# A fixed instruction list is replaced by another: merged exponentials, work moved to GpSimd, another loading order

## The chip, the cores and the metric

The kernel runs on one core of a Trainium2 chip. The metric is the device time of one execution in microseconds (us). Three runs of the kernel before took 295.99, 296.73 and 299.36 us; the median is 296.73.

## The reference

One transformer layer on 2048 tokens of width 640, bfloat16. Attention has 32 heads of width 20 and goes through four segments of 512 tokens. Each segment combines ordinary causal softmax attention inside the segment with a read from a memory matrix that earlier segments have filled; then comes an MLP with hidden width 1728.

```
x -> layernorm -> q, k, v = x@wq, x@wk, x@wv          (32 heads of 20)
phi(t) = t + 1 if t > 0 else exp(t);  g = sigmoid(beta)
for each segment s of 512 tokens:
    a_dot = softmax(q k^T * 20**-0.5 + causal mask) v
    a_mem = (phi(q) M) / (phi(q) z + 1e-6)
    o[s]  = g * a_mem + (1 - g) * a_dot
    M += phi(k)^T v ;  z += sum(phi(k))
h   = x + o @ wo
out = h + silu(layernorm(h) @ w1) @ w2
```

## The kernel before

All work is cut into named tasks. Each task is a few instructions on one engine. The order of the tasks is not computed in the kernel: it stands in a long text, `ORDER`, which names one task after another. `Graph.schedule` walks through it. An entry reads `name/engine:slots`. The engine letter is A (ScalarE, ACT), D (VectorE, DVE), G (GpSimd, POOL) or S (SP, which issues the DMAs); without a letter the first engine that the task allows is taken. The letter C on a TensorE task means the same matmuls cut into four column tiles of 32 (line 549) instead of the whole array (line 548). The numbers are buffer slots; for the pool `ps` they are PSUM banks, of which there are eight. Every engine carries out its own tasks in the order of the list. A tracker puts a semaphore wait wherever a task reads or overwrites what another engine made. So a task that waits holds up everything behind it on its engine, and the list is the whole plan.

The tasks by name, with s the segment, c one of five blocks of packed heads, b one of 16 blocks of 128 tokens, k = 8s + g the group of four heads:

- `x0` to `x12`, `w_...`: loads of tokens and weights; `re_...` rearranges query and key weights into the packed form; `fillN` is N small matmuls on zeros.
- `n1_stb`, `n1_rsb`, `n1_apb`: layer-norm statistics (line 753; on ACT lines 744 to 748), reciprocal root on GpSimd (763, 765) and application (781). For the first segment the result is transposed by TensorE (`n1_tp`, 791) and copied (`n1_te`, 800), later by a transposing DMA (`n1_tr`). `n2_...` is the same before the MLP.
- `prscw` (548, 549) projects queries (w = 0) or keys (w = 1), `qescw` evicts (876, 877). `ex` (883), `pa` (the clamp max(t, 0) + 1, line 890) and `pb` (896) make phi. `vt` are DMAs that bring the heads of groups 5 to 7, split over the blocks, together (the virtual heads).
- `v`, `ve`: value projection and its eviction (842, 843).
- `qk{k}a`, `qk{k}b`, `qk{k}e`: a score visit, eight or four matmuls in four row tiles (946) into four banks, two pairs. `e{k}a0` and `e{k}a2` are the exponentials of the two pairs (959). `mk` sets the upper triangle of the diagonal blocks to zero on GpSimd (971).
- `av` multiplies by the values (994, "PV product" below), `oe` evicts with the gate (1008 on ACT, 1010 on DVE), `tm` and `td` bring memory and local result to token order, `nm` normalizes (1058 to 1064), `ad` adds the two (1072, GpSimd).
- `kt`, `mz`, `ma`, `mb`: the memory update.
- `ot`, `wo`, `rs`: output projection and residual; `h1` and `th` (1211), `s` (1217): first MLP product and SiLU through tanh; `h2`, `o` (1254), `out`: second product, last addition, store.

In the list the MLP of segment s runs between the score visits of segment s + 1 and s + 2, so that TensorE has matmuls to do while ACT works through the exponentials. The last segment's MLP stands alone at the end.

The exponential of a pair is one instruction over two banks:

```
def e_ex(eng, q0=q0, scp=scp):
    b0 = scp.slot
    T.add(AC, lambda e: e.activation(out=pt[:, pta.slot, q0:q0 + 2, 0:width],
                                     in_=sc3[:, b0:b0 + 2, 0:width], func=ACT.Exp, scale=SCALE), ...)
```

Of the kernel before, what the change touches and what calls it, by code (L numbers as in the profile page):

```python
# [6 lines left out]
ALU = mybir.AluOpType  # L7
# [220 lines left out]
class Task:  # L228
    __slots__ = ("name", "engs", "emit", "reads", "writes", "prio", "mode", "allocs", "preds", "npred",
                 "succ", "ready", "lat", "start", "end", "eng", "idx", "bw", "cols", "alt")  # L230
# [4 lines left out]
class Graph:  # L235
# [15 lines left out]
    def task(self, name, engs, emit, reads=(), writes=(), prio=0.0, mode=None, reserve=(), lat=None, bw=0.0, alt=False):  # L251

        t = Task()
        t.cols, t.alt = False, alt
# [33 lines left out]
    def schedule(self):  # L288
# [3 lines left out]
        for row in ORDER:  # L292
# [18 lines left out]
            for a in t.allocs:  # L311
# [7 lines left out]
            for a in t.allocs:  # L319
                a.users -= 1  # L320
# [54 lines left out]
pr030.1/C qe040/D pa031:0 av0:3 pb021 mk1a qe030/D mm1 n1_tr7 vt05 oe0/D:0 qk2e0:6,4 vt010 mk1b av1:2 e2b2 epsg1 mk2b
pb041 mk2a td0/C:3 e2e2:5 e2e0 oe1/D:1 qk3a0:4,0 nm0:3,0 vt07 e3a2:6 v10.0:2 td1:6 nm1:2 vt011 e3a0 v10.1 ve10/D:1
qk3b0:0,6 e3b2:4 e3b0 mm7 n1_st9:2 mk2e av2:3 mk3a oe2/D:1 qk4a0:6,4 e4a2:3 v11.0/C:2 e4a0 v11.1/C qk4b0:0,4 td2/C:6
epsg0 ve11/D pb031 mk3b nm2:2 mtb3 av3:7 e4b0:1 vt01 e4b2 vt02 n1_rs9 oe3/D:0 mzc1 n1_st10:7 vt08 n1_st8:1 vt04
qk4e0:2,0 mk4a pr100.0/C:4 e4e2:4 pr100.1/C qe100/D:0 pa100:0 qk5a0:0,6 pr110.0/C:5 pr110.1/C e4e0 qe110/D:0 e5a0:5
w_wo/S:0 qk5b0:2,0 pr120.0/C:4 pr120.1/C qe120/D:0 mk4b e5a2 mk4e av4:5 oe4/D:1 mk5a kt02:0 pa120:0 e5b2:2 qk6a0:0,6  # L380
n1_rs8 td3/C:4 n1_ap8:0 nm3:0 e5b0 mk5b v12.0:2 v12.1 kt04:4 ve12/D e6a0:1 ex120:0 e6a2 w_w2_3/S td4:1 ex100:1 mz01:0
mz00 mm8 mz04 mz02 kt03:1 n1_rs10 n1_ap10:3 mz03 ma0/D:0 qk6b0:4,2 e6b2:0 e6b0 mk6b nm4:3 pr101.0:7 pr101.1 qk6e0:0,2
e6e2:6 qe101/D av5:6 pr111.0/C:7 pr111.1/C e6e0 qk7a0:4,2 mk6e w_w2_0/S mk6a e7a0:4 e7a2 n1_tr8:1 mk7a oe5/D:0 qe111/D
td5:6 pr130.0/C:0 pr130.1/C nm5:1 n1_tr10 qk7b0:6,4 e7b2:5 e7b0 mk7b n1_ap9:0 qe130/D:0 n1_st11:7 v13.0:1 mm3 v13.1/C
ve13/D ex101:2 n1_rs11 av6:0 qk8a0:3,6 e8a0:3 pa101:0 e8a2 pr140.0:5 pr140.1/C av7:4 oe6/D:1 mzc3 qk8b0:0,2 w_w1_4/S
td6/C:6 e8b0:2 w_w1_3/S n1_tr9 mzc5 pb101 kt10:1 qe140/D:0 oe7/D:0 mk8a nm6:2 pr131.0/C:7 td7/C:4 nm7:1 mzc7 mzc4
ot0:0 qk8e0:5,0 pr131.1/C ot1 n1_ap11:1 mm0 qe131/D pr121.0:4 pr121.1 pa130:0 pa110:0 ot2 qe121/D vt19:0 pa131:1 mzc0
e8b2 mk8b e8e0:5 w_w2_4/S mzc2 qk9a0:5,2 pb100 e8e2 mk8e pr141.0:7 pr141.1 qe141/D pa121:0 e9a2:4 qk9b0:0,2 e9a0 pb120
pa111:2 wo0.0/C:4 wo0.1/C rs0 e9b0:6 av8:7 e9b2 vt12 mk9b ot3 ex110:0 wo1.0/C:0 qk10a0:3,5 oe8/D:0 n1_tr11 vt16
n2_st0:1 vt10 e10a0:3 wo1.1 rs1 n2_st1:6 mb00:0 mm11 vt13 e10a2 wo2.0:2 wo2.1 rs2 ex111:2 pb111 n2_st2:0 mk10a  # L390
qk10b0:6,0 e10b2:0 vt11 wo3.0/C:4 wo3.1/C qk10e0:2,0 rs3 vt15 n2_rs1 e10b0 vt14 v21.0:6 e10e2:2 vt18 n2_ap1:0 n2_st3:6
e10e0 v21.1 ve21/D:0 mm9 qk11a0:4,0 e11a0:1 mm6 n2_tr1:0 v20.0/C:2 v20.1/C n2_rs0 v22.0/C:4 n2_rs2 tm8/C:6 td8/C
ex131:2 ex130:1 n2_ap2:3 ve20/A n2_tr2 v22.1/C e11a2 mk10b pb110 pr201.0/C:2 n2_rs3 n2_ap3:1 n2_tr3 nm8:0,1 n2_ap0:2
n2_tr0 ex121:0 mk9a pb130 av9:3 ve22/A qk11b0:6,0 e11b0:5 pr201.1 qe201/D:0 oe9/D:1 v23.0:4 v23.1 mk10e mb02:0 av10:2
e11b2 mb01:0 ve23/A qk12a0:0,6 mzc8 td9:4 pb121 ex141:0 tm9 pa140:0 vt110 e12a2:4 pr211.0:3 pr211.1 oe10/D:0 td10:6
e12a0 tm10 h1_0_0_0.0:2 qe211/A:0 mk11a pb131 h1_0_0_0.1 th0_0_0:0 ad8:0 nm9:0,1 mk11b mzc6 qk12b0:3,0 mb03:0 e12b2:0
nm10:1,0 av11:5 s0_0_0:0 h1_0_1_0.0/C:6 e12b0 h1_0_1_0.1/C kt11:4 pa141:2 pr221.0/C:7 vt111 vt17 qk12e0:2,0 w_w2_1/S
th0_1_0:0 pr221.1 oe11/D:1 tm11:4 td11 s0_1_0 ex140:1 e12e0:2 h1_0_2_0.0:6 h1_0_2_0.1 pb141 kt14:0 qe221/D:0 e12e2
# [924 lines left out]
```

## Time and profile before

| | |
|---|---|
| runs | 295.99, 296.73, 299.36 us |
| span of the profiled execution, first to last instruction | 293.9 us (the median of the runs is 2.8 above it; no separate time is listed for the profiled execution) |
| PE busy | 282.0 us (96%), 4365 matmuls |
| weight loads (PEld) | 159.8 us (54%) |
| DVE busy | 218.6 us (74%), 456 instructions |
| ACT busy | 216.5 us (74%), 281 |
| POOL busy | 148.1 us (50%), 294 |
| chain that ended last | PE 83%, DVE 7%, ACT 6%, DMA 1%, issue 1% |
| granted TensorE clock | full |

The page gives busy time by engine, then the span in 40 slices, the DMA queues, the chain of work that ended last, and groups of instructions with their mean duration and what ended the idle time before them. Matmuls are pipelined, and a matmul's recorded length covers its way through the array, so PE counts as busy over short waits. A wait is put down to the engine that released it last; "issue" means that the trace shows nothing that was waited for.

### The profile page before, as it was taken

To read this page: it belongs to the slowest core of one execution; us is meant where nothing else is said; L and a number is where in the kernel's file an instruction comes from. 1 tells how busy PE (TensorE), PEld (TensorE's weight loads), DVE (VectorE), ACT (ScalarE), POOL (GpSimd) and SP (SyncE) were. 2 spreads that over 40 slices of the span, in tenths; PEclk is the share of its full clock that TensorE was granted. 3 is DMA by queue.
4 is the path that set the end of the run, shared out by engine and by line. 5 is a ranking of instruction groups with operands and counts; after the bars stand their busy time and mean duration, and the time that the engine had idled before them with its cause. 6 is when DMAs were issued, how large, how long until landed. Compare 5 with 4: busy or idle time off the path is not lost.

```text
span 293.9 us, 10138 instructions
## 1 busy us (share of the span) xinstructions
PE 282.0 (96%) x4365; PEld 159.8 (54%) x4365; DVE 218.6 (74%) x456; ACT 216.5 (74%) x281; POOL 148.1 (50%) x294
## 2 busy tenths in 40 slices
PE   6899889999999999999999899999999999999996
PEld 5454435445644445566654554656664657754574
DVE  3999888899997678798899835877746776635613
ACT  7699999999999899977789857979979640005400
POOL 6759675686947545746748432348638321300000
PEclk9999999999999999999999999999999999999999
DMA  7947869635464200453543402403320031450003
GB/s 212 342 120 186 113 176 186 167 69 108 87 80 113 73 2 3 53 99 70 91 122 92 93 2 21 81 2 57 73 25 2 2 70 22 91 156 0 3 0 112
DMA packets 48604, 24.83 MB, mean 84 GB/s; under 512 B 38896, under 2 KB 47472, under 8 KB 48560
## 3 DMA queue, kind: packets, MB, share of 16 engines
q1 hardware_dynamic: 48560, 24.19, 38.1%
q8 instruction: 34, 0.56, 0.8%
q14 instruction: 10, 0.08, 0.1%
HBM read 10.41 MB, written 2.62 MB: 44 GB/s over the span
## 4 chain that ended last, share of the span: by engine, by line
PE 83%; DVE 7%; ACT 6%; DMA 1%; issue 1%; POOL 0%; SPq 0%; ACTq 0%; DVEq 0%
PE ps_all L548 49%; PE ps_all L549 20%; PE ps_all L946 8%; ACT PT L959 5%; PE ps_all L994 5%; DMA x_tok<-in_A_x_dram 1%; PE ps_all L1198 1%; DVE xn_rot L781 1%; DVE oTs L1010 1%; DVE phiQ L890 1%; DVE stt L753 1%; PE ps_all L1112 1%; DVE Vx L843 1%; DVE otok L1046 1%; DVE QK L877 0%
## 5 line engine op out<-in xcount | busy, mean ns | idle before, releaser
L959 ACT ACTIVATE PT<-ps_all 128x1024 bf16<-128x1024 f32 x160 | 154.1, 1027 | 16.2 <-PE ps_all L946 15.1
L971 POOL TENSOR_SCALAR_AFFINE_SELECT PT<-PT 128x512 bf16<-128x512 bf16 x128 | 82.8, 651 | 63.9 <-ACT PT L959 60.5
L1211 ACT ACTIVATE th<-ps_all 128x512 f32<-128x512 f32 (+1 forms) x56 | 31.7, 589 | 38.1 <-PE ps_all L548 23.7
L1217 DVE SCALAR_TENSOR_TENSOR sT<-th,ps_all 128x512 bf16<-128x512 f32 (+1 forms) x56 | 36.0, 661 | 17.0 <-ACT th L1211 16.4
L548 PE MATMUL ps_all<-w_sb,sT 128*128 128x320 bf16 x324 | 46.3, 299 | 0.1
L548 PE MATMUL ps_all<-tT,w_sb 128*128 128x512 bf16 x178 | 41.4, 380 | 0.0
L548 PEld LDWEIGHTS ps_all<-w_sb,sT 128*128 128x128 bf16 x324 | 31.0, 98 | 13.2 <-issue 0.6
L753 DVE BATCH_NORM_STATS2 stt<-x_tok 128x6 f32<-128x320 bf16 x62 | 27.1, 478 | 3.8 <-DMA x_tok<-in_A_x_dram 3.6
L1072 POOL TENSOR_TENSOR otok<-on 128x320 bf16<-128x320 bf16 x24 | 19.7, 824 | 17.5 <-DVE on L1064 17.5
L1254 DVE SCALAR_TENSOR_TENSOR x_tok<-ps_all,x_tok 128x640 bf16<-128x640 f32 (+1 forms) x17 | 13.3, 784 | 17.9 <-PE ps_all L548 13.1
L548 PEld LDWEIGHTS ps_all<-tT,w_sb 128*128 128x128 bf16 x178 | 16.5, 98 | 18.7 <-issue 0.6
L877 DVE CAST QK<-ps_all 128x512 bf16<-128x512 f32 x25 | 17.1, 685 | 8.6 <-PE ps_all L548 4.7
L1010 DVE TENSOR_SCALAR oTs<-ps_all,lsc 128x512 bf16<-128x512 f32 x26 | 19.3, 741 | 2.6 <-PE ps_all L994 2.2
L549 PE MATMUL ps_all<-tT,w_sb 128*32 128x512 bf16 x328 | 20.5, 380 | 0.0
L1064 DVE TENSOR_TENSOR on<-ps_all,rd 128x640 bf16<-128x640 f32 x24 | 19.8, 824 | 0.8
L765 POOL TENSOR_TENSOR rst<-rst,eps_c 128x1 f32<-128x1 f32 x32 | 18.3, 573 | 2.5
L549 PE MATMUL ps_all<-w_sb,sT 128*32 128x320 bf16 x496 | 18.8, 300 | 0.0
L781 DVE TENSOR_SCALAR xn_rot<-x_tok,mvt,rst 128x640 bf16<-128x640 bf16 x31 | 16.1, 534 | 3.3 <-POOL rst L765 2.8
L548 PE MATMUL ps_all<-tT,wkr 128*128 128x512 bf16 (+1 forms) x77 | 18.4, 367 | 0.0
L548 PE MATMUL ps_all<-wv_sb,tT 128*128 128x320 bf16 x115 | 18.0, 300 | 0.5 <-ACT PT L959 0.3
L763 POOL TENSOR_TENSOR rst<-mvt,eps_c 128x1 f32<-128x1 f32 x32 | 6.7, 209 | 22.5 <-DVE mvt L756 21.8
L994 PE MATMUL ps_all<-PT,Vx 128*32 128x512 bf16 (+3 forms) x384 | 17.4, 301 | 0.0
(111 smaller groups left out, 403.1 us busy)
## 6 DMA issues: line engine op xcount, KB each, us to landing
out_dram<-x_tok SPq DMA_DIRECT2D x15, 160.0 KB, 1.9
w_sb<-in_B_w_dram SPq DMA_DIRECT2D x5, 432.0 KB, 4.1
x_tok<-in_A_x_dram SPq DMA_DIRECT2D x3, 640.0 KB, 4.4
w_sb<-in_B_w_dram SPq DMA_DIRECT2D x3, 480.0 KB, 4.0
QKV<-QK SPq DMA_DIRECT2D x12, 72.0 KB
wv_sb<-in_A_wv_dram SPq DMA_DIRECT2D x1, 800.0 KB, 8.2
wo_sb<-in_A_wo_dram SPq DMA_DIRECT2D x1, 800.0 KB, 5.3
w_sb<-in_B_w_dram SPq DMA_DIRECT2D x1, 640.0 KB, 6.0
```

What stands on the lines that cost most here:

```text
L548: return [lambda e: e.matmul(out, lhsT=lhsT, rhs=rhs, start=start, stop=stop)]
L549: return [lambda e, p=p: e.matmul(out[p:p + 32, :], lhsT=lhsT[:, p:p + 32], rhs=rhs, start=start, stop=stop, tile_position=(0, p)) for p i ...
L753: T.add(DV, lambda e, hh=hh: e.bn_stats(out=stt[:, s, 6 * hh:6 * hh + 6], in_=xb[:, 320 * hh:320 * hh + 320]), reads=R((xa, xsub)), writes ...
L946: fns.append(lambda e, j=j, o=o, r=r, q0=q0, q1=q1, qa=qa, ka=ka: e.matmul(ps_all[:, o:o + q1 - q0], lhsT=ka[32 * r:32 * r + DH, 128 * j:1 ...
L959: T.add(AC, lambda e: e.activation(out=pt[:, pta.slot, q0:q0 + 2, 0:width], in_=sc3[:, b0:b0 + 2, 0:width], func=ACT.Exp, scale=SCALE), re ...
L971: fns.append(lambda e, v=v: e.affine_select(out=v, in_=v, pattern=[[0, 4], [1, 128]], compare_op=ALU.is_ge, fill=0.0, base=0, channel_mult ...
L994: fns.append(lambda e, j=j, r=r, h=h, pa=pa, pt=pt, co=co, q0=q0, ji=ji: e.matmul(bank(po)[32 * r:32 * r + 32, q0:hi], lhsT=vtile(vx)[:, j ...
L1010: f = lambda e: e.tensor_scalar(out=o, in0=i_, scalar1=lsc[:, g:g + 1], scalar2=None, op0=ALU.mult)
L1064: T.add(DV, lambda e: e.tensor_tensor(out=on[:, ona.slot, :, :].rearrange("p b (x e) -> p b x e", e=DH), in0=v[:, :, :, 0:DH], in1=r2.unsq ...
L1072: T.add(PO, lambda e: e.tensor_tensor(out=o_dst, in0=on[:, ona.slot, 0, :].rearrange("p (i x) -> p i x", i=4), in1=on[:, ona.slot, 1, :].r ...
L1211: T.add(AC, lambda e: e.activation(out=th[:, tha.slot, lo:hi], in_=bank(ps)[:, lo:hi], func=ACT.Tanh, scale=0.5), reads=R((ps, [0])), writ ...
L1217: T.add(DV, lambda e: e.scalar_tensor_tensor(out=sT[:, f, lo:hi], in0=th[:, tha.slot, lo:hi], scalar=1.0, in1=bank(ps)[:, lo:hi], op0=ALU. ...
```

## The change

The list is another one from the first entry to the last. What it uses and the code now offers:

- 19 score visits have one exponential over all four banks instead of two over a pair each. The letter W on one of the two tasks takes the other in; the pairs are then sorted by bank, and one access pattern with the distance between them reads both.
- Clamps `pa` and applications `n1_ap`, `n2_ap` may run on GpSimd. In the list 16 of 30 clamps and 15 of 32 applications do. The ACT form of the very first application, with its extra GpSimd instruction for the bias, is gone.
- The leading fillers are 20 and 5 instead of 25 and 5.
- Entries with C for TensorE are 283 instead of 116.
- The loads at the start come in another order: x block 0, blocks 2 and 3, block 1, key weights, query weights, beta, value weights; before: blocks 0, 1, 2 and 3, query weights, key weights, value weights, beta.

The same matrix products are computed. The core of the diff, with the two lists cut to their first lines:

```diff
@@ schedule
-            t.cols = eng == "C"
-            t.eng = {"A": AC, "D": DV, "G": PO, "S": SP, "C": PE}[eng] if eng else list(t.engs)[0]
+            t.cols, t.whole = eng == "C", eng == "W"
+            t.eng = {"A": AC, "D": DV, "G": PO, "S": SP, "C": PE, "W": AC}[eng] if eng else list(t.engs)[0]
+            both = [t]
+            if t.whole:
+                m = todo.pop(name[:-1] + ("2" if name[-1] == "0" else "0"))
+                both.append(m)
...
@@ ORDER
-epsc:0 iota halfc zpad warm:0 x0:0 mt2 n1_st0:4 mt3 mt0 mt1 mta1 mtb1 vpad1 x1:1 n1_st1/A:1,2 x2:2,3 w_q0:0 w_q1 w_k0
-vpad0 fill25:0 n1_rs0 n1_ap0/A:1 sel n1_tp0:2 fill5:7 n1_te0/A:1 n1_st2/D:5,3 mta0 n1_rs1 n1_st3:0 n1_rs2 w_k1 w_wv:0
...
+zpad:0 x0:1 vpad1 warm:0 mt1 mta1 iota n1_st0:1 sel x2:7,0 n1_st2:7,0 fill20:7 mt2 epsc mta2 mtb2 mt3 mta3 mm10 halfc
+n1_rs0 mt0 n1_ap0/G:1 fill5:6 n1_st3:0 x1:2 n1_st1/A:2,2 n1_rs1 n1_tp0:3 n1_te0:2 n1_ap1 n1_tp1:0 n1_te1 n1_rs2 n1_ap2
+n1_tp2:4 n1_te2 n1_rs3 n1_ap3:2 n1_tp3:6 n1_te3 w_k1:0 w_k0 re_wk3/G:0 re_wk1/G mtb3 mm11 re_wk0 pr001x.0/C:2 w_q1
...
@@ layer_norm
-            if eng == AC:
-                T.add(AC, lambda e: e.activation(out=xn_rot[:, xn.slot, :], in_=x_tok[:, b % 12, :], func=ACT.Identity,
-                                                 scale=rst[:, s, :], bias=nmr[:, s, :]),
...
-        G.task(f"{tag}ap{b}", {DV: 0.46, AC: 0.70} if first else {DV: 0.46}, e_apply,
+        G.task(f"{tag}ap{b}", {DV: 0.46, PO: 0.88}, e_apply, [(xa, xsub), (st, ["mv", "r"])], [(xn, [0])], prio)
...
@@ declare_front
-                    G.task(f"pa{s}{c}{w}", {DV: 0.37}, e_pa, [(qk[c], wall)], [(pa, ["a"])], prp)
+                    G.task(f"pa{s}{c}{w}", {DV: 0.37, PO: 0.7}, e_pa, [(qk[c], wall)], [(pa, ["a"])], prp)
...
@@ scores
+                        if any(t.whole for t in ets):
+                            a, b = rank()
+                            src = bass.AP(tensor=ps_all, offset=512 * a.slot,
+                                          ap=[[4096, 128], [512 * (b.slot - a.slot), 2], [512, 2], [1, width]])
+                            o = pt[:, pta.slot, 0:4, 0:width].rearrange("p (a b) x -> p a b x", a=2)
+                            T.add(AC, lambda e: e.activation(out=o, in_=src, func=ACT.Exp, scale=SCALE), ...)
+                            return
```

(The numbers in braces in the code are the planner's costs; the fixed list does not read them.)

More of the change, by code (lines that the diff above doesn't have):

```diff
@@ L229 @@
     __slots__ = ("name", "engs", "emit", "reads", "writes", "prio", "mode", "allocs", "preds", "npred",
-                 "succ", "ready", "lat", "start", "end", "eng", "idx", "bw", "cols", "alt")
+                 "succ", "ready", "lat", "start", "end", "eng", "idx", "bw", "cols", "alt", "whole")
 class Graph:
@@ L253, in task @@
         t = Task()
-        t.cols, t.alt = False, alt
+        t.cols, t.alt, t.whole = False, alt, False
         t.name, t.emit, t.mode, t.lat, t.bw = name, emit, mode, lat, bw
@@ L318, in schedule @@
             assert not slots, name
-            for a in t.allocs:
-                a.users -= 1
+            for q in both:
+                for a in q.allocs:
+                    a.users -= 1
             order.append(t)
@@ L733, in layer_norm @@
         xn = G.alloc("xn")
-        first = tag == "n1_" and b < 1
         if tag == "n1_":
@@ L766, in e_rstd @@
                   reads=R((st, ["r"]), (C, ["half"])), writes=R((st, ["r"])))
-            if first:
-                T.add(PO, lambda e: e.tensor_scalar(out=nmr[:, s, :], in0=mvt[:, s, 0:1], scalar1=rst[:, s, :], scalar2=-1.0,
-                                                    op0=ALU.mult, op1=ALU.mult),
-                      reads=R((st, ["mv", "r"])), writes=R((st, ["n"])))
-        G.task(f"{tag}rs{b}", {PO: 0.83}, e_rstd, [(st, ["mv"]), (C, ["eps", "half"])],
-               [(st, ["r", "n"] if first else ["r"])], prio)
+        G.task(f"{tag}rs{b}", {PO: 0.83}, e_rstd, [(st, ["mv"]), (C, ["eps", "half"])], [(st, ["r"])], prio)
         def e_apply(eng):
             s = st.slot
-            if eng == AC:
-                T.add(AC, lambda e: e.activation(out=xn_rot[:, xn.slot, :], in_=x_tok[:, b % 12, :], func=ACT.Identity,
-                                                 scale=rst[:, s, :], bias=nmr[:, s, :]),
-                      reads=R((xa, xsub), (st, ["r", "n"])), writes=R((xn, [0])))
-                return
-            T.add(DV, lambda e: e.tensor_scalar(out=xn_rot[:, xn.slot, :], in0=x_tok[:, b % 12, :],
-                                                scalar1=mvt[:, s, 0:1], scalar2=rst[:, s, :],
-                                                op0=ALU.subtract, op1=ALU.mult),
+            T.add(eng, lambda e: e.tensor_scalar(out=xn_rot[:, xn.slot, :], in0=x_tok[:, b % 12, :],
+                                                 scalar1=mvt[:, s, 0:1], scalar2=rst[:, s, :],
+                                                 op0=ALU.subtract, op1=ALU.mult),
                   reads=R((xa, xsub), (st, ["mv", "r"])), writes=R((xn, [0])))
-        G.task(f"{tag}ap{b}", {DV: 0.46, AC: 0.70} if first else {DV: 0.46}, e_apply,
-               [(xa, xsub), (st, ["mv", "r", "n"] if first else ["mv", "r"])], [(xn, [0])], prio)
+        G.task(f"{tag}ap{b}", {DV: 0.46, PO: 0.88}, e_apply, [(xa, xsub), (st, ["mv", "r"])], [(xn, [0])], prio)
         if tag == "n1_" and b < 4:
@@ L955, in scores, with e_ex @@
                     scp = sca[(q0 - r0) // 2]
-                    def e_ex(eng, q0=q0, scp=scp):
+                    def e_ex(eng, q0=q0, scp=scp, rank=rank, ets=ets):
+                        if any(t.whole for t in ets):
+                            a, b = rank()
+                            src = bass.AP(tensor=ps_all, offset=512 * a.slot,
+                                          ap=[[4096, 128], [512 * (b.slot - a.slot), 2], [512, 2], [1, width]])
+                            o = pt[:, pta.slot, 0:4, 0:width].rearrange("p (a b) x -> p a b x", a=2)
+                            T.add(AC, lambda e: e.activation(out=o, in_=src, func=ACT.Exp, scale=SCALE),
+                                  reads=[("ps", z.slot + q) for z in (a, b) for q in range(2)], writes=R((pta, [0, 2])))
+                            return
                         b0 = scp.slot
```

215 lines of the change are left out of this document (111 added, 104 removed).

## The prediction

> **What bounds the kernel now.** I began with the page (span, engines, chain), went to the busy time by stretch, then to the chain in order of time, and last to single groups and to the first 14 us.
>
> ```profile
> span 293.9 us, 10138 instructions
> ...
> PE 282.0 (96%) x4365; PEld 159.8 (54%) x4365; DVE 218.6 (74%) x456; ACT 216.5 (74%) x281; POOL 148.1 (50%) x294
> ...
> PE 83%; DVE 7%; ACT 6%; DMA 1%; issue 1%; POOL 0%; SPq 0%; ACTq 0%; DVEq 0%
> ```
>
> TensorE is 96% busy and is 83% of the chain that ended last. The matmuls' amount does not change, so I ask where TensorE stands still. I cut the span at the first score visit (13.47), at the visits of groups 8 and 17, and behind the last group's PV product, and call the five stretches rows one to five. Columns: PE, weight loads, DVE, ACT, POOL busy; clock; DMA.
>
> ```profile
> 0.00:13.47 13.47, 9.87 (x75) 6.85 (x76) 8.25 (x33) 9.50 (x16) 9.46 (x36) 1.00 0.86 266
> 13.47:57.61 44.14, 40.78 (x713) 20.47 (x713) 39.31 (x87) 42.22 (x52) 29.95 (x65) 1.00 0.78 169
> 57.61:118.12 60.51, 59.69 (x1135) 30.57 (x1132) 52.05 (x107) 57.42 (x74) 39.02 (x74) 1.00 0.33 65
> 118.12:231.90 113.78, 112.31 (x2038) 65.07 (x2039) 85.64 (x174) 94.33 (x119) 64.37 (x109) 1.00 0.32 57
> 231.90:293.90 62.00, 59.39 (x416) 36.81 (x412) 33.35 (x60) 13.05 (x24) 5.32 (x11) 1.00 0.20 54
> ```
>
> The granted clock is full everywhere. PE idles 3.36 us in the second row, 0.82 in the third, 1.47 in the fourth; the 2.6 of the last row is the closing add and store. ACT is 96% and 95% busy in rows two and three: there PE and ACT are both at their limit, and PE's waits are ACT's length showing through. So at most 5.65 us of visible idle can go, plus waits under some 0.15 us that pipelined matmuls cover in this view, plus changes of PE's mode. Those I price from the chain (start, length):
>
> ```profile
> 37.24 3.79 ACT PT L959 x4
> ...
> 42.76 1.19 PE ps_all L549 x20
> 43.95 0.33 PE ps_all L946 x8
> ...
> 63.91 1.19 PE ps_all L548 x5
> ...
> 104.63 2.27 PE ps_all L549 x40
> ...
> 291.33 0.49 DVE x_tok L1254
> ```
>
> Five 512-column steps ahead of a visit take 1.19, ten take 2.27: five more cost 1.08, so one change of mode costs 0.11. Whole-array (L548) and four-column-tile form (L549) cost the same, 1.19 each.
>
> **The change, part by part.**
>
> *Mode changes and column tiles.* In the two written lists PE changes mode 173 times before and 165 after: 8 x 0.11 = -0.9 us (bounds -1.0, and 0 if a wait fills the place). The tail turns to column tiles almost throughout, at the same price per step. But each step is then four matmuls: 4365 become 6397.
>
> *Fillers.* 20 and 5 in place of 25 and 5; they end before the transposes need PE. 0, since the chain below waits for data.
>
> *Merged exponentials.* Prices by group (mean ns):
>
> ```profile
> L959 ACT ACTIVATE PT<-ps_all 128x1024 bf16<-128x1024 f32 x160 | 154.1, 1027 | 16.2 <-PE ps_all L946 15.1
> L971 POOL TENSOR_SCALAR_AFFINE_SELECT PT<-PT 128x512 bf16<-128x512 bf16 x128 | 82.8, 651 | 63.9 <-ACT PT L959 60.5
> ...
> L1211 ACT ACTIVATE th<-ps_all 128x512 f32<-128x512 f32 x52 | 30.3, 604 | 35.6 <-PE ps_all L548 23.7 <-DVE sT L1217 11.4 <-PE ps_all L549 0.4
> ...
> L1072 POOL TENSOR_TENSOR otok<-on 128x320 bf16<-128x320 bf16 x24 | 19.7, 824 | 17.5 <-DVE on L1064 17.5
> ...
> L781 DVE TENSOR_SCALAR xn_rot<-x_tok,mvt,rst 128x640 bf16<-128x640 bf16 x31 | 16.1, 534 | 3.3 <-POOL rst L765 2.8 <-DVE sT L1217 0.4
> L883 ACT ACTIVATE ex<-QK 128x512 bf16<-128x512 bf16 x25 | 15.5, 630 | 1.2 <-DVE phiQ L896 1.2
> ...
> L890 DVE TENSOR_SCALAR phiQ<-QK 128x512 bf16<-128x512 bf16 x15 | 7.1, 491 | 0.1
> ...
> L1008 ACT ACTIVATE oTs<-ps_all,lsc 128x512 bf16<-128x512 f32 x6 | 4.1, 690 | 0.1
> ...
> L711 POOL COPY wkr<-sT 128x400 bf16<-128x400 bf16 x2 | 1.1, 563 | 1.3 <-DMA sT<-in_A_wk_dram 1.3
> ```
>
> 512 more elements cost 1027 - 604 = 423 ns, so 1024 more cost 846 and a merged exponential 1.87. Two in a row cost 1.95: four take 3.79, hence 0.92 each and 1.03 the last. Saved: 0.08. Upper bound the whole fixed part, 1027 - 846 = 0.18; lower bound -0.1, since a merged one starts after all eight matmuls (0.33 a visit) and frees no bank at half time. I take 0.08: 19 x 0.08 = 1.5 us of ACT, two in row two, seven in row three, ten in row four.
>
> *Moves on ACT.* The list shifts three clamp exponentials (L883) out of row two, one to before it and two into row three: with the merges, row two loses 3 x 0.6 + 0.16 = 2.0, row three gains 2 x 0.6, one eviction (L1008, 0.69) and loses 0.56: +1.3. Row four gains two evictions and loses ten times 0.08, +0.6, where ACT has 19 idle: nothing. Of row two's 2.0 I count half, since DVE (39.31 of 44.14) and the masks then end last: **-1.0** (bounds -2.0, +2.0). Row three: PE has only 0.82 idle, ACT 3.1; **+0.2** (-0.8, +1.3).
>
> *Clamps and applications on GpSimd.* 16 clamps and 15 applications leave DVE: 16 x 0.49 + 14 x 0.53 = 15 us of 218.6 (the fifteenth application was on ACT). On GpSimd no such row exists. Lower bounds: the select (651 ns for 512), 0.65 and 0.81; upper: the two-input add (824 for 320), 1.32 and 1.65. Both are one-input operations like the copy (563 for 400), so I take 0.72 and 0.90: +25 us on an engine with 146 idle. That is nothing on the path where masks keep their lead over the PV products, and 2 to 4 us where they lose it (a rival). For DVE the relief counts in row four, where it frees 6 clamps and 9 applications, 7.7 of 85.64.
>
> DVE's own clamps and applications are uneven:
>
> ```profile
> L781 DVE TENSOR_SCALAR xn_rot<-x_tok,mvt,rst x31: 433/442/911, 7.9 to 257.2; 128x640 bf16<-128x640 bf16 x31
> ```
>
> Minimum 433, longest 911. The Trainium skill, "SBUF — State Buffer", section "Who interferes with whom", says that such a DVE operation and a GpSimd instruction hold a shared port pair exclusively, the loser blocking wholly. The spread agrees with it but no row names the blocker. By that rule a busier GpSimd delays what stays on DVE; by the mean row it does not. With half of the 31 stretched by 0.47 the sum would lose 7 of DVE's 15, and the rival below gains weight.
>
> *Row four.* Its idle holds one stop in the middle of a visit:
>
> ```profile
> 168.80 0.23 PE L946 MATMUL ps_all<-QKV 20*128 20x128 bf16 x3 [0.88 <-issue]
> ```
>
> Nothing in the trace released it; I read it as instructions that had not arrived. It need not fall on a dense place again: I count half, -0.45. Of the other 0.59 and the covered small waits I take -1.05, because DVE has 7.7 us more room. Row four: **-1.5** (-2.5, +1.5).
>
> *The head.* SP's loads are ordered anew: block 1 of x after blocks 2 and 3, key weights before query weights.
>
> ```profile
> 3.59 0.74 ACT L744 ACTIVATE xn_rot<-x_tok 128x640 bf16<-128x640 bf16 x1 [0.23 <-DMA x_tok<-in_A_x_dram]
> 5.61 0.92 ACT L777 ACTIVATE xn_rot<-x_tok,nmr,rst 128x640 bf16<-128x640 bf16 x1
> 5.88 0.88 DVE L753 BATCH_NORM_STATS2 stt<-x_tok 128x6 f32<-128x320 bf16 x2 [1.56 <-DMA x_tok<-in_A_x_dram]
> ...
> 8.08 0.32 POOL L763 TENSOR_TENSOR rst<-mvt,eps_c 128x1 f32<-128x1 f32 x1 [0.18 <-DVE mvt L756]
> ...
> 9.22 0.45 DVE L781 TENSOR_SCALAR xn_rot<-x_tok,mvt,rst 128x640 bf16<-128x640 bf16 x1 [0.51 <-POOL rst L765]
> 9.73 0.45 PE L791 MATMUL ps_all<-ident,xn_rot 128*128 128x128 bf16 x5 [0.51 <-DVE xn_rot L781]
> 10.08 0.71 PE L548 MATMUL ps_all<-tT,wqr 128*128 128x256 bf16 x5
> 10.45 1.06 POOL L711 COPY wkr<-sT 128x400 bf16<-128x400 bf16 x3 [1.33 <-DMA sT<-in_A_wk_dram]
> 13.47 0.39 PE L946 MATMUL ps_all<-w_sb 20*128 20x512 bf16 x4
> ```
>
> Today block 1 is there at 3.59 and its statistics on ACT end at 5.61 (2.02). Loaded third it lands when the third load does, 5.88, and ends at 7.9. On GpSimd the reciprocal roots of blocks 1, 2 and 3 stand behind it in order, 0.8 each (8.08 to 9.12 with the gap to L781): 10.3. The last application ends at 10.75 and its transposes at 11.2, where today they end at 10.18. First projection 11.1 against 10.08; the query weights, now the last of the four to land, come near 10.45 and are hidden. The same projections stand before the first visit in both lists: 14.6 against 13.47, **+1.1** (bounds +0.4 if block 1 lands with x's bytes at once, +1.8 if an early rearrangement is late too).
>
> *SP's queue otherwise.* The loads of blocks 4 to 11 come as two issues in a row right behind the attention weights, and the output weight's load now stands ahead of the copies of the virtual heads, which group 5 is the first to need. One issue more in that queue is covered by the visits of groups 0 to 4; without that cover group 5's first visit would wait as long as the issue takes. 0.
>
> **Sum:** +1.1 - 0.9 - 1.0 + 0.2 - 1.5 = -2.1. Span 293.9 - 2.1 = 291.8. The median of the runs is 296.73, 2.8 above the span, and that stays: **294.6 us**.
>
> **Rivals.**
>
> *The list closes nearly all gaps.* All 5.65 of idle but a floor of 0.5, and 0.9 of mode changes, against +1.1: -5.0, **291.8**. For it: half of DVE's relief falls where PE waits; against it: row two has every engine near its limit.
>
> *Masks come late (slower).* Place: groups 2 to 5, row two, where GpSimd does its work in order.
>
> ```profile
> 37.43 1.34 POOL L971 TENSOR_SCALAR_AFFINE_SELECT PT<-PT 128x512 bf16<-128x512 bf16 x2 [1.38 <-ACT PT L959]
> 42.92 1.34 POOL L971 TENSOR_SCALAR_AFFINE_SELECT PT<-PT 128x512 bf16<-128x512 bf16 x2 [0.50 <-ACT PT L959]
> ...
> 39.41 0.72 PE L994 MATMUL ps_all<-PT,sT 128*32 128x512 bf16 x16
> 45.30 0.72 PE L994 MATMUL ps_all<-PT,sT 128*32 128x512 bf16 x16
> ```
>
> ```profile
> 13.47:45.30 31.83, 28.85 (x433) 14.09 (x436) 28.48 (x65) 30.58 (x38) 23.04 (x52) 1.00 0.72 166
> ```
>
> Masks end at 38.77 and 44.26; the PV products that need them start at 39.41 and 45.30, a lead of 0.64 and 1.04. Up to 45.30 GpSimd idles 31.83 - 23.04 = 8.8 us, of which the two waits shown for exponentials, 1.9, stay: 6.9 of room. The new list puts three clamps and three applications more there: 3 x 0.72 + 3 x 0.90 = 4.9 us at my prices, 8.9 at the upper bounds. It decides once the six cost over 6.9. At the upper bounds 2.0 reach PE in place of row two's -1.0; row three then gives its upper bound and row four nothing, since what DVE sheds comes back late: 1.1 - 0.9 + 2.0 + 1.3 + 0 = +3.5, **300.2**. Against it: the nearest row, the copy, puts the prices in the lower half.
>
> *Instructions come late (slower).*
>
> ```profile
> q8 instruction: 34, 0.56, 0.8%
> ```
>
> 34 blocks today and one stop of 0.88; 6397 matmuls make 50. Were one in eight late, 6 x 0.9 = 5.4 in place of 0.9: -2.1 + 5.0 = +2.9, **299.6**. The Trainium skill, "Runtime: NRT & Kernel Launch", section "Instruction fetch mechanics", calls the refill mostly hidden; by it this costs nothing, by the row some 1.3 (50/34 x 0.88). The row decides.
>
> *It does not do what it says.* A merged exponential saves nothing, gaps move elsewhere, the head costs its 1.1: -0.9 + 1.1 + 0.3 = +0.5, **297.2**.
>
> **How the numbers follow.** Forecast 0.36, gaps closed 0.27, masks 0.18, instructions 0.07, no effect 0.12. One per cent, 2.97 us, is about what a measurement of this kernel can tell from no change. Faster by more: all but 0.01 of the gaps case and 0.14 of the forecast, 0.40. Slower by more: 0.14 of the masks, 0.05 of the instructions, 0.05 of the others with several upper bounds at once, 0.24. Within: 0.36. Range 290.0 to 300.6: from beyond the gaps case to the masks case.
>
> **What would show it.** Right: first visit near 14.6; PE idle in the second stretch about 2.4 and in the fourth under 1; merged exponentials near 1.87; GpSimd clamps near 0.72, applications near 0.90; tail of the same length. Wrong: PV products waiting for L971's successor, or stops released by "issue" above 2 us together, or a first visit before 13.8.

## The result, and the profile after

The changed kernel takes 333.19 us (median of four runs, 330.38 to 334.49), the old one 297.14 beside it: ratio 1.118, 95% interval [1.111, 1.126]. The forecast was 294.6, the range 290.0 to 300.6. The change costs 36 us where 2 were to be gained.

From the page of the kernel after: span and busy times, the TensorE clock by slices of 8.3 us, the chain.

```profile
span 331.0 us, 14171 instructions
...
PE 295.2 (89%) x6397; PEld 170.9 (52%) x6397; DVE 207.8 (63%) x427; ACT 217.0 (66%) x266; POOL 212.0 (64%) x318
...
PEclk9599679999999999999979997999978999999999
...
PE 42%; POOL 30%; ACT 13%; DVE 6%; DMA 4%; issue 3%; SPq 1%; POOLq 0%; DVEq 0%; ACTq 0%
```

GpSimd rose from 148.1 to 212.0 us and from 0% to 30% of the chain. TensorE is busy 13 us longer with the same matrix products, and its clock row, 9 throughout before, has holes. The busy time by stretch, cut at the same tasks as in the prediction (first score visit, visits of groups 8 and 17, behind the last PV product); columns PE, weight loads, DVE, ACT, POOL busy, clock, DMA:

```profile
0.00:16.89 16.89, 12.56 (x145) 8.35 (x146) 8.68 (x29) 9.41 (x18) 11.48 (x36) 0.80 0.83 268
16.89:70.39 53.50, 43.66 (x832) 21.23 (x829) 37.59 (x88) 41.91 (x49) 42.79 (x73) 0.90 0.54 122
70.39:135.86 65.47, 60.40 (x1353) 31.02 (x1350) 49.84 (x98) 57.69 (x69) 53.27 (x77) 1.00 0.33 55
135.86:270.00 134.14, 120.23 (x2538) 69.49 (x2542) 79.82 (x160) 94.46 (x110) 96.90 (x124) 0.95 0.31 54
270.00:331.00 61.00, 58.37 (x1547) 40.80 (x1536) 31.91 (x56) 13.55 (x24) 7.58 (x12) 1.00 0.30 52
```

Against before: +3.42, +9.36, +4.96, +20.36, -1.00, together the span's 37.1. The groups (busy, mean ns) show why:

```profile
L970 ACT ACTIVATE PT<-ps_all 128x1024 bf16<-128x1024 f32 x122 | 117.4, 1031 | 41.7 <-PE ps_all L949 39.6 <-POOL PT L982 1.4
L982 POOL TENSOR_SCALAR_AFFINE_SELECT PT<-PT 128x512 bf16<-128x512 bf16 x128 | 82.5, 651 | 40.9 <-ACT PT L970 26.5 <-ACT PT L966 11.1
...
L778 POOL TENSOR_SCALAR xn_rot<-x_tok,mvt,rst 128x640 bf16<-128x640 bf16 x15 | 37.9, 2530 | 1.0
L966 ACT ACTIVATE PT<-ps_all 128x2048 bf16<-128x2048 f32 x19 | 35.7, 1881 | 6.6 <-PE ps_all L949 6.4
...
L886 POOL TENSOR_SCALAR phiK<-QK 128x512 bf16<-128x512 bf16 x8 | 15.3, 1919 | 0.0
```

A merged exponential takes 1.88 us, as reckoned (1.87). An application on GpSimd takes 2.53 where 0.90 was assumed, a clamp 1.92 where 0.72 was; the 31 moved instructions make 68.6 us (37.9 + 16 x 1.92), not 25. What this does to TensorE is plain in row two, first in GpSimd's order, then in TensorE's (start, length, idle time ahead and its releaser):

```profile
31.72 2.50 POOL L778 TENSOR_SCALAR xn_rot<-x_tok,mvt,rst 128x640 bf16<-128x640 bf16 x1
34.18 1.94 POOL L982 TENSOR_SCALAR_AFFINE_SELECT PT<-PT 128x512 bf16<-128x512 bf16 x3
36.09 1.93 POOL L886 TENSOR_SCALAR phiK<-w_sb 128x512 bf16<-128x512 bf16 x1
```

```profile
36.26 1.26 PE L1005 MATMUL ps_all<-PT,sT 128*32 128x512 bf16 x16 [3.35 <-POOL PT L982]
37.28 1.09 PE L557 MATMUL ps_all<-tT,wqr 128*32 128x512 bf16 x8
41.56 0.62 PE L949 MATMUL ps_all<-w_sb 20*128 20x256 bf16 x8 [3.19 <-DVE w_sb L873]
```

The first PV product waits 3.35 us for masks that stand behind an application. Sixteen such matmuls then take 1.26 us where they took 0.72 before, and the clock column shows why:

```profile
32.00:36.00 4.00, 0.91 (x16) 0.20 (x16) 0.00 (x0) 2.35 (x3) 3.93 (x4) 0.99 0.72 213
36.00:46.00 10.00, 6.55 (x100) 2.94 (x104) 6.26 (x14) 3.67 (x4) 8.18 (x14) 0.50 0.38 69
46.00:50.00 4.00, 3.28 (x68) 1.76 (x61) 3.13 (x7) 3.16 (x5) 2.22 (x5) 0.98 0.28 43
```

One stop of 3.35 us is followed by some 10 us at half clock. The Trainium skill, "TensorE: Matmul & The Clock Gate", Part 1, states that after at least one idle window of about 3.4 us the array runs at half rate until it has been busy for such a window; this stop agrees, and the last section has a shorter one that was enough.

A label misleads once: one of the longest stops, before a projection of segment 3, is put down to "issue".

```profile
199.16 0.86 PE L556 MATMUL ps_all<-tT,wqr 128*128 128x512 bf16 x3 [3.75 <-issue]
```

```profile
193.97 2.50 POOL L778 TENSOR_SCALAR xn_rot<-x_tok,mvt,rst 128x640 bf16<-128x640 bf16 x1
```

Its operand tT is the transpose of block 15, whose application, the last of four on GpSimd, ends at 196.47; the transpose lands some 2.6 us later, at 199.1, and TensorE starts at 199.16. By these times it is GpSimd's wait, and no late instruction.

### The profile page after: what moved, and what is told of

Its sections match the earlier page's. It is cut to its first block, busy times and chain, and to the rows that moved or that the text cites. A ratio compares the mean times of both kernels' runs of the same rounds, so it can differ in the third digit from the quotient of the medians.

```text
span 331.0 us, 14171 instructions
## 1 busy us (share of the span) xinstructions
PE 295.2 (89%) x6397; PEld 170.9 (52%) x6397; DVE 207.8 (63%) x427; ACT 217.0 (66%) x266; POOL 212.0 (64%) x318
## 4 chain that ended last, share of the span: by engine, by line
PE 42%; POOL 30%; ACT 13%; DVE 6%; DMA 4%; issue 3%; SPq 1%; POOLq 0%; DVEq 0%; ACTq 0%
PE ps_all L557 32%; POOL xn_rot L778 9%; ACT PT L970 8%; POOL PT L982 8%; PE ps_all L556 4%; POOL rst L772 4%; POOL phiK L886 3%; PE ps_all L949 3%; PE ps_all L1005 3%; POOL phiQ L886 2%; ACT PT L966 2%; POOL Mzb L1150 2%; DVE stt L760 1%; POOL rst L770 1%; DMA phiKt<-phiK 1%
## 5 line engine op out<-in xcount | busy, mean ns | idle before, releaser
L970 ACT ACTIVATE PT<-ps_all 128x1024 bf16<-128x1024 f32 x122 | 117.4, 1031 | 41.7 <-PE ps_all L949 39.6
L1222 ACT ACTIVATE th<-ps_all 128x512 f32<-128x512 f32 (+1 forms) x56 | 31.7, 588 | 35.1 <-PE ps_all L557 26.2
L557 PE MATMUL ps_all<-w_sb,sT 128*32 128x320 bf16 x1456 | 54.4, 304 | 0.0
L557 PEld LDWEIGHTS ps_all<-w_sb,sT 128*32 128x32 bf16 x1456 | 39.3, 98 | 12.4 <-issue 2.0
L557 PE MATMUL ps_all<-tT,w_sb 128*32 128x512 bf16 x724 | 43.6, 379 | 0.0
L966 ACT ACTIVATE PT<-ps_all 128x2048 bf16<-128x2048 f32 x19 | 35.7, 1881 | 6.6 <-PE ps_all L949 6.4
L778 POOL TENSOR_SCALAR xn_rot<-x_tok,mvt,rst 128x640 bf16<-128x640 bf16 x15 | 37.9, 2530 | 1.0
L557 PEld LDWEIGHTS ps_all<-tT,w_sb 128*32 128x32 bf16 x724 | 18.4, 97 | 16.4 <-issue 0.9
L557 PE MATMUL ps_all<-tT,wqr 128*32 128x512 bf16 (+1 forms) x336 | 22.8, 397 | 0.1
L1021 DVE TENSOR_SCALAR oTs<-ps_all,lsc 128x512 bf16<-128x512 f32 x23 | 17.2, 747 | 8.4 <-PE ps_all L1005 8.4
L557 PE MATMUL ps_all<-tT,wkr 128*32 128x512 bf16 (+1 forms) x316 | 21.2, 395 | 0.5 <-DVE x_tok L1187 0.5
L556 PE MATMUL ps_all<-tT,w_sb 128*128 128x512 bf16 x79 | 19.1, 380 | 0.0
```

The source lines that it names most:

```text
L556: return [lambda e: e.matmul(out, lhsT=lhsT, rhs=rhs, start=start, stop=stop)]
L557: return [lambda e, p=p: e.matmul(out[p:p + 32, :], lhsT=lhsT[:, p:p + 32], rhs=rhs, start=start, stop=stop, tile_position=(0, p)) for p i ...
L778: T.add(eng, lambda e: e.tensor_scalar(out=xn_rot[:, xn.slot, :], in0=x_tok[:, b % 12, :], scalar1=mvt[:, s, 0:1], scalar2=rst[:, s, :], o ...
L966: T.add(AC, lambda e: e.activation(out=o, in_=src, func=ACT.Exp, scale=SCALE), reads=[("ps", z.slot + q) for z in (a, b) for q in range(2) ...
L1222: T.add(AC, lambda e: e.activation(out=th[:, tha.slot, lo:hi], in_=bank(ps)[:, lo:hi], func=ACT.Tanh, scale=0.5), reads=R((ps, [0])), writ ...
```

## The experiments

Times are medians; ratios are to the old kernel on the same chip, with 95% intervals.

**First: is it GpSimd, and which of the two operations?** In the new list `/G` was turned into `/D` for all, for the applications, for the clamps; and in the old list the same tasks, but for the first block's application, were turned to `/G`.

```
e1:  n1_ap5/G:0 -> n1_ap5/D:0 ...   pa011/G:1 -> pa011/D:1 ...     (15 + 16 entries)
e2:  applications only               e3:  clamps only
e4:  old list: n1_ap5:0 -> n1_ap5/G:0 ...   (14 + 16 entries)
```

> The new list with all 16 clamps and 15 applications given back to DVE, everything else as in the new kernel. Theory 'GpSimd price': a clamp takes 1.92 us and an application 2.53 us on GpSimd (profile after), 68.6 us in all where 25 were reckoned, so masks and transposes come late; with them back the time falls to 293 to 299 us, near the forecast. Rival 'the list itself': the new order, its head and the merged exponentials cost most of the 36 us, and the time stays above 312 us.

> Only the 15 applications go back to DVE; the 16 clamps stay on GpSimd. GpSimd price: 37.9 of the 68.6 us leave GpSimd, and if the loss goes by its time, 36 us x 37.9/68.6 = 20 us return: about 313 us. If applications hurt more because transposes and projections hang on each, 300 to 306 us. The list itself: above 320 us.

> Only the 16 clamps go back to DVE; the 15 applications stay on GpSimd. GpSimd price, by its time: 36 x 30.7/68.6 = 16 us return, about 317 us. If applications carry most of the loss: 325 us or more. The list itself: above 320 us as well, so it is told apart by the run with all back.

> The old list, in which the same 16 clamps and 14 of the 15 applications (without the first block's, which stays on ACT) run on GpSimd at their old places; nothing else of the change. GpSimd price: the old list, too, loses tens of us, 320 to 340. The list itself: the old order has room for them on GpSimd (146 us idle), and the time stays within 303 us.

All back: 332.9 us (1.119 [1.110, 1.128]). Applications back: 334.0 (1.125 [1.117, 1.134]). Clamps back: 323.8 (1.090 [1.083, 1.097]). Old list with the moves: 336.8 (1.133 [1.126, 1.140]).

The old list loses 40 us by the moves alone, so they are enough for the whole loss. There TensorE's PV products wait for masks ten times, 21.6 us together (total, times, longest):

```profile
PE ps_all L994 <- POOL PT L971: 21.6, 10, 3.8
```

But the new list loses as much without the moves, which by the expectation speaks for the rival, and the parts miss too: applications back brought nothing where 20 us were expected, clamps back 9 where 16 were. Each reading alone is too simple. In the run with all back TensorE's stops that DVE ends add up to 17.2 us, 4.3 in the old kernel. One wait shows how they come about (DVE, then TensorE):

```profile
248.31 0.82 DVE L1265 SCALAR_TENSOR_TENSOR x_tok<-ps_all,x_tok 128x640 bf16<-128x640 f32 x1 [1.50 <-PE ps_all L557]
249.06 0.88 DVE L778 TENSOR_SCALAR xn_rot<-x_tok,mvt,rst 128x640 bf16<-128x640 bf16 x1
```

```profile
252.73 2.32 PE L557 MATMUL ps_all<-tT,w_sb 128*32 128x512 bf16 x20 [4.47 <-issue]
```

This application (block 10) has had its reciprocal root since 221.57. On GpSimd its place in the list means "behind the masks"; on DVE the same place means "behind the residual addition `o7`", which waits for TensorE. It starts 27 us late, its transpose is issued at 249.96 and lands 2.6 us later, and TensorE stands for 4.47 us. Giving back at the same places makes new waits, so it is no clean control.

**Second: the price alone.** All 31 stay on GpSimd at their places, as plain copies (the clamp's and the normalization's arithmetic is left out); and the operations are measured by themselves.

```
e5: on GpSimd only: tensor_scalar(out, in, ...) -> tensor_copy(out, in)
e6: old kernel + 16 GpSimd instructions at the end of the list, on scratch tiles
e7: e1, each entry moved up to the first place behind its input
e8: e5, e1b2/W:3 -> e1b2:3 e1b0 ... (19 visits)
```

> The new list as it is, with its 31 moved instructions on GpSimd at their places, but each of them a plain copy of the same operand into the same tile (the clamp's and the normalization's arithmetic on GpSimd is left out). The copy of 400 elements took 563 ns, so about 0.72 and 0.90 us, the prices that the forecast assumed, in place of the measured 1.92 and 2.50. Theory 'only the price was wrong': every other step of the sum holds, and the time is 292 to 300 us. Rival 'the list has other faults' (head, order of the DVE, merged exponentials): above 308 us, as with all given back to DVE (332.9).

> The old kernel with 16 more GpSimd instructions behind its last one, on scratch tiles nobody reads: two each of tensor_scalar with max and add by constants on 512 and on 256, with max alone, with add alone, with subtract and mult by constants, with subtract and mult by per-partition scalars on 640, a copy of 512 and a two-input add of 512. Theory 'two arithmetic stages cost': one stage near 0.7 to 1.0 us, two stages 1.9. Rival 'any tensor_scalar on GpSimd costs 3.75 ns an element': one stage 1.9 too. Rival 'contention in the new kernel made them long': two stages 0.7 to 0.9 here, where DVE is half idle. Time of the kernel: as before, within 1 us.

> All 31 given back to DVE as in the run that took 332.9 us, but each entry moved up in the list to the first place behind its input where its slot is free. Theory 'DVE works in order': given back at the places that were meant for GpSimd, applications and clamps stood behind DVE entries that wait for TensorE; moved up, 305 to 318 us. Rival 'the new list is bad on any engine': 328 us or more.

> As the run with copies on GpSimd, but the 19 merged exponentials are each split again into two over two banks. Theory of the prediction: a merged one saves 0.08 us of ACT; split, the time is the same to 1 us longer. Rival: a merged one starts only after all eight matmuls and frees no bank at half time, so split is 1 to 4 us shorter.

With copies: 305.3 us (1.026 [1.022, 1.029]), the application's copy 0.72. So 28 of the 36 us are the price of GpSimd's arithmetic, with all that hangs on it, and some 8 are something else: more than the theory allowed, less than the rival asked. The prices by themselves, on a GpSimd with nothing else to do (two of each):

```profile
261.97 3.94 POOL L627 TENSOR_SCALAR bn<-bn 128x512 bf16<-128x512 bf16 x2
265.99 3.06 POOL L628 TENSOR_SCALAR bn<-bn 128x512 bf16<-128x512 bf16 x2
269.13 2.22 POOL L627 TENSOR_SCALAR bn<-bn 128x256 bf16<-128x256 bf16 x2
271.45 5.12 POOL L627 TENSOR_SCALAR bn<-bn,bs 128x640 bf16<-128x640 bf16 x2
276.63 1.28 POOL L633 COPY bn<-bn 128x512 bf16<-128x512 bf16 x2
278.00 2.16 POOL L634 TENSOR_TENSOR bn<-bn 128x512 bf16<-128x512 bf16 x2
280.25 3.07 POOL L628 TENSOR_SCALAR bn<-bn 128x512 bf16<-128x512 bf16 x2
283.40 3.94 POOL L627 TENSOR_SCALAR bn<-bn 128x512 bf16<-128x512 bf16 x2
```

L627 has two arithmetic stages, L628 one (max in the second line, add in the seventh). On 512 elements a copy takes about 0.61, a two-input add 1.04, one stage 1.49, two stages 1.92; two stages on 256 take 1.07, per-partition scalars on 640 take 2.51. Contention is out: these are the same prices as in the new kernel. Both other theories were half right: one stage is dear already, and a second adds 0.43. The kernel's time, 299.6, is a single run, 2.0 above the median of the old kernel beside it; at most 1 was expected.

Moved up, all on DVE: 329.8 (1.103 [1.097, 1.110]), far from the 305 to 318 expected and where the rival put it. TensorE's stops that DVE ends add up to 26.2 us. The first place behind the input is no good place either: a clamp whose slot in phi(k) was still held by a transpose stopped DVE for 4.91 us, and the eviction behind it held TensorE.

```profile
91.03 0.29 DVE L927 TENSOR_SCALAR phiK<-QK 128x512 bf16<-128x512 bf16 x1 [4.91 <-DMA phiKt<-phiK]
```

So the new list is not bad as such, as the run with copies shows; whether it works with these tasks on DVE in some other order stays open.

Split exponentials: 307.4 (1.032 [1.028, 1.036]) against 305.3: the 19 merges bring some 2 us in the new list, more than the 0 to 1 expected, though the two intervals touch.

**Third: the other 8 us.** In the run with copies TensorE stands still from 6.5 to 9 us and its clock is 0.50 behind that; with more fillers it is full (9 to 15 us, copies first, fillers second):

```profile
9.00:15.00 6.00, 5.66 (x87) 3.90 (x91) 3.98 (x14) 3.72 (x9) 3.48 (x11) 0.50 0.88 293
```

```profile
9.00:15.00 6.00, 5.55 (x127) 3.89 (x124) 4.90 (x17) 4.33 (x10) 3.99 (x12) 1.00 0.89 299
```

```
e10: e5, fill20 -> fill26, fill16 behind n1_tp0, fill4 behind n1_tp1
e11: e5, x1:2 moved up behind x0:1
e13: both
e12: old list, 17 visits merged: e7b2:5 e7b0 -> e7b2/W:5 ...
```

> The run with copies on GpSimd (305.3 us), with 26 leading fillers instead of 20, and 16 and 4 more between the first transposes, so that TensorE does not stand still from 6.5 to 9 us. Theory 'clock': in the runs with the new list the granted clock is 0.50 from 9 to 15.5 us, because TensorE stood still ahead of it, and the first projections run at half speed; with fillers it stays near 1.00, first visit near 14.8 instead of 16.8, time 302 to 304 us. Rival 'the data are late': the clock stays full, and the first visit moves by less than 0.5 us.

> The run with copies on GpSimd (305.3 us), with block 1 of x loaded right behind block 0 again, ahead of blocks 2 and 3; nothing else. The prediction's head: block 1 loaded third costs 1.1 us, so the time falls to about 304; if TensorE then also stands still for less long and keeps its clock, to 302. Rival 'loads do not bind': 305, first visit at 16.8.

> Both edits of the head together: block 1 loaded second and 26, 16 and 4 fillers. If head and clock are all that the new list loses beside GpSimd's price: 297 to 299 us. If what is left lies in the later stretches (they gave 5 to 6 us more than the forecast in the run with copies): 301 to 303, first visit 13.5 to 14.5.

> The old list with 17 of its score visits given one exponential over four neighbouring banks, placed where the first of the two stood; nothing else of the change. Theory of the prediction: 0.08 us of ACT saved each, 1.4 in all, half of it on the path: 296 to 297 us against 297.5. Rival 'freeing no bank at half time': 299 to 302 us.

Fillers: first visit at 14.86 instead of 16.82, time 302.8 (1.018 [1.013, 1.024]). Load order: first visit 15.50, time 304.6 (1.024 [1.019, 1.029]). Both: 14.50, time 302.2 (1.015 [1.009, 1.021]). The clock theory holds in the head. The two edits together bring some 3 us, no less than the 2.3 that the first visit gains; for the load order alone the interval does not tell a gain from none. But 297 to 299 us were expected if the head and the clock were all that is lost beside GpSimd's price, so more is lost later. The kernel with fillers shows a stop that the run with copies does not have (SP's queue, the chain, TensorE):

```profile
42.31 2.31 SPq L592 DMA_DIRECT2D w_sb<-in_B_w_dram  x4
44.66 1.23 SPq L1116 DMA_TRANSPOSE phiKt<-phiK  x1
45.94 1.26 SPq L592 DMA_DIRECT2D w_sb<-in_B_w_dram  x1
47.24 1.68 SPq L804 DMA_TRANSPOSE tT<-xn_rot  x1
48.97 2.60 SPq L1116 DMA_TRANSPOSE phiKt<-phiK  x1
```

```profile
48.97 7.75 DMA phiKt<-phiK
```

```profile
56.76 0.54 PE L1127 MATMUL ps_all<-sT,phiKt 128*32 128x42 bf16 x48 [2.29 <-DMA phiKt<-phiK]
```

The new list puts weight loads ahead of the transposes kt03 (four) and kt04 (one more). kt04 is issued at 48.97, is 7.75 us on its way beside the loads, and TensorE waits 2.29 for it.

Merged in the old list: 301.8 (1.016 [1.013, 1.019]), 5 us slower, by the rival of that expectation. A pair's banks are free after 1.03 us, a merged visit's after 1.88, and in that list the next visit of TensorE has to wait for them. TensorE's waits for these exponentials rise from 1.7 us in the old kernel to 6.0; an example from the chain:

```profile
50.14 1.89 ACT PT L976
52.03 0.14 issue
52.16 0.40 PE ps_all L959 x8
```

**Fourth: the queue, and the real arithmetic.**

```
e14: e13, "kt02:2 w_w2_3 w_w1_2 w_w2_0 w_w1_0 kt03:4 w_w1_3 n1_tr9:1 kt04:3" ->
          "kt02:2 kt03:4 w_w2_3 n1_tr9:1 kt04:3", the other loads ahead of mz01
e15: the new kernel with the edits of e13 and e14, arithmetic on GpSimd
```

> The run with copies on GpSimd and the repaired head (302.2 us), with four of the five weight loads that the new list puts ahead of the fourth and fifth transposes of the keys' features (kt03, kt04) put behind them again in SP's queue. In that run the transpose kt04 is issued at 49.41 us and lands 7.5 us later, and TensorE stands still for 3.45 us at mz04. Theory 'SP's queue': the stop goes, time 298 to 300 us. Rival 'the wait moves': something else of the second stretch is late next, and the time stays at 301.5 or more.

> The new kernel with its real arithmetic on GpSimd, and the same repaired head and queue. Theory 'GpSimd bounds it': masks and applications end when GpSimd is through its list, whatever TensorE gains ahead of them, so 326 to 333 us against 333.2. Rival 'the terms add': 333.2 - 3.1 - 3 = 327 or less.

With the queue mended: 299.45 us (1.007 [1.004, 1.011]); the stop at mz04 is gone. The interval touches that of the run before it (1.009 to 1.021), so the gain of 2.7 rests on the stop that is no longer in the trace as much as on the times. With the real arithmetic the same edits bring 2.6 us, 330.6 (1.109 [1.103, 1.116], against [1.111, 1.126] without them, so hardly clear of noise), where they brought 5.9 with copies: most of it is hidden behind GpSimd, as expected. No version beat the old kernel.

## Why the prediction was wrong

By steps, against the run with copies, head and queue mended (e14), which is nearest to the forecast's world:

```profile
0.00:14.70 14.70, 12.55 (x171) 9.42 (x171) 8.05 (x29) 9.45 (x18) 9.86 (x36) 1.00 0.83 268
14.70:60.41 45.71, 40.10 (x827) 20.47 (x828) 38.76 (x88) 42.03 (x49) 33.22 (x73) 1.00 0.62 137
60.41:121.22 60.81, 58.93 (x1346) 31.44 (x1348) 50.22 (x98) 57.40 (x68) 41.99 (x77) 1.00 0.38 73
121.22:236.60 115.38, 112.24 (x2526) 66.78 (x2534) 80.93 (x160) 94.08 (x110) 73.27 (x124) 1.00 0.35 63
236.60:297.80 61.20, 58.51 (x1555) 40.74 (x1544) 32.15 (x56) 13.60 (x24) 6.01 (x12) 1.00 0.24 52
sum 297.80, PE 282.32 PEld 168.85 DVE 210.11 ACT 216.55 POOL 164.36; mean PE 56.46 PEld 33.77 DVE 42.02 ACT 43.31 POOL 32.87
```

- *Clamps and applications on GpSimd*: the step that failed. The price was taken from the copy, and the "upper bound" from the two-input add was none: 1.32 and 1.65 against 1.92 and 2.53. The rival "masks come late" named the place, the mechanism and the decision point (6.9 us for six moved operations before 45.30); they cost 13.4 (3 x 1.92 + 3 x 2.53). It put the price at 300.2, since it capped the loss with the false bound, and stopped at the queue of masks: transposes waiting for applications, and the clock, were not in it. The step's price: 28 us, with the clock that it costs (e5).
- *Fillers at 0*: wrong as soon as TensorE's data come later than the fillers end. The row "clock 1.00 everywhere" was read as a constant of the kernel; it was a result of its having no long stop. In the new kernel TensorE is busy 295.2 us where e14, at full clock, needs 282.3: 13 us of its span's 37 are slow matmuls.
- *The head*: +1.1 forecast, +3.42 measured. The step itself holds. At full clock the first projection starts at 11.10 (e10; 11.1 forecast) and the first visit is 1.39 later than before. With block 1 second again and nothing else (e11) the first projection starts at 10.16, in the run with copies at 11.30: 1.14 for the load order. What the sum left out is the half clock and, in the new kernel, the first application on GpSimd, for which TensorE waits 1.86. In e13 the load order moves the first visit by only 0.36 (14.50 against 14.86), but there the sixteen fillers hold block 1's transposes until 9.12, though its application is done by 8.5.
- *SP's queue otherwise, 0*: wrong. I weighed the token loads that moved and overlooked five weight loads ahead of kt04: a stop of 2.29 us in e10. The run with copies, whose head is slower, has no such stop.
- *Merged exponentials*: duration right (1.88). In the new list they gain 2 us for 19, near the 1.5 reckoned on ACT; in the old one they lose 5 us for 17, 0.3 a visit, beyond the lower bound of 0.1. That the gain comes near the sum is therefore partly luck: it depends on the list around it.
- *Column tiles* at the same price: right (the lists as written have 121 entries with C before and 279 after). TensorE's busy time in e14 is 282.3 with 6408 matmuls, 26 more fillers among them, before 282.0 with 4365. The tail was to keep its length; it shrank by about 1 us, both in the changed kernel and in e14 (61.0 and 61.2 against 62.0).
- *"Instructions come late"*: 50 blocks are fetched, as reckoned, but the long stops read by their waits are GpSimd, DMA and DVE. Stops put down to "issue" add up to 2.3 us in e14 against 0.9 before, but to 2.7 in e12 too, which has the old number of matmuls. No run varied the instructions alone.
- *Rows two and four, -1.0 and -1.5*: with the price and the queue mended they are +1.6 and +1.6 (45.71 and 115.38 against 44.14 and 113.78). So some 5 us between e14 and the forecast (299.45 against 294.6; 297.8 against 291.8 by spans) stay unexplained; the gaps that DVE's relief was to close moved elsewhere, and no run tells where from. *Mode changes* (-0.9) were not tested by themselves.

## What to carry to other kernels

An operation that the profile does not show on an engine has no price yet: neither the nearest row nor a heavier-looking one bounds it, and an idle engine at the end of the program is a place to measure it for the cost of a few scratch instructions. In a list with strict order per engine, moving a task to another engine also moves it into another queue: ask what stands ahead of it there, for every engine and every DMA queue. The full clock of a profile holds for a kernel without long stops; where a change can make a stop of some 3 us, add the time at half clock behind it.

## What the runs showed of the hardware

- GpSimd's tensor_scalar with two stages on bfloat16 costs an estimated 3.3 ns per element of a partition and 0.2 us (from 1.92 at 512 and 1.07 at 256), where DVE's clamps took 0.41 to 0.50 at 512 on the average before. The Trainium skill, "GPSIMD Engine Reference", section "4.1 Engine selection", calls one-input operations there roughly line-rate and two-input ones about twice as slow as on VectorE; here the two-input add (1.04) is faster than one-input arithmetic (1.49 and 1.92), and only the copy (0.61 at 512, 0.72 at 640) fits. The measurement decides.
- A busier GpSimd did not stretch the applications that stayed on DVE: median 447 ns in the new kernel, 442 before (means 524 and 534). DVE's step `pb` did get longer, 554 and 478 ns for queries and keys where it took 460 and 453. But in the run with all back, with GpSimd busy for 145.1 us, it took 649 and 497, so these runs do not put it down to GpSimd's load.

```profile
L778 DVE TENSOR_SCALAR xn_rot<-x_tok,mvt,rst x17: 393/447/780, 8.8 to 289.7; 128x640 bf16<-128x640 bf16 x17
```

- Half clock lasts some 10 us after the stop of 3.35, in part because the second stop falls into it. In the run with copies a shorter stop was enough: TensorE stands for 2.47 us and has 0.53 us of work in the three us ahead of the stretch at 0.50.

```profile
6.00:9.00 3.00, 0.53 (x8) 0.35 (x7) 0.82 (x3) 1.89 (x6) 1.40 (x4) 0.98 1.01 322
```

- The old kernel loses some clock too in part of its executions: of the 13 beside e14, the eight at a mean clock of 0.999 or 1.000 took 295.3 to 298.0 us, the five at 0.993 or 0.994 took 298.5 to 299.2.
